# Batch 0 of a block-attention and mixture-of-experts kernel: normalising on GpSimd, an earlier Q load, a later V sum

## The chip, the cores and the metric

One core of one Trainium2 chip. The metric is device time in microseconds of one execution. Engines are named as in the profile: PE (TensorE, its weight loads PEld), DVE (VectorE), ACT (ScalarE), POOL (GpSimd), SP (SyncE, which here only issues DMAs).

## The reference

Three layers, one after another, all in float32:

```python
def attention(q, k, v):                       # (2, 8, 768, 64) each
    k_sum = k.reshape(B, H, 24, 32, D).max(axis=3)      # one summary key per block of 32
    v_sum = v.reshape(B, H, 24, 32, D).mean(axis=3)     # one summary value per block
    scores_l = scale * q @ k.T   where |i - j| < 16, else -1e9
    scores_s = scale * q @ k_sum.T + log(32)
    a = softmax(concat([scores_l, scores_s]))           # exp, divided by (sum + 1e-9)
    return a @ concat([v, v_sum])
x = attention(q, k, v) as (1536, 512)
x = (silu(x @ w_gate) * (x @ w_val)) @ w_out            # d_ff 1536
out = moe2(x)    # 8 experts, top 1, gated: relu(x @ w1[e]) @ w2[e] for each token's expert
```

## The kernel before

Attention runs over sub-blocks s of 64 queries, 12 for each batch. For one sub-block: `att_sm` (line 210) multiplies Q by 96 near keys and 24 summary keys into a PSUM tile S; `att_se` (line 221) runs four pairs of a DVE instruction (mask and row minimum, line 228) and an ACT exponential with its row sum (line 231), giving e; `att_n` (line 235) adds 1e-9 to the sums, takes the reciprocal and multiplies e by it (lines 238 to 240, all on DVE); `att_t` (line 242) transposes e on PE into PT and copies it to pt with ACT; `att_v` (line 252) multiplies by 96 rows of V and 24 rows of V sums that stand under them in the tile vx, and ACT and DVE split the result PV into xh and xl, the transposed input of the dense layer. e has three buffers, so the mask instruction of sub-block s waits for the transposes of s-3.

The order of all this is written out by hand. For batch 0 it is `start` (line 851): loads of six K tiles and three Q tiles; six K stages with filler transposes; three 512 KB loads of V for its block sums (`vs_load`); then the first attention steps, and a loop of 15 turns i in which sub-block i gets its exponentials, i-1 is normalised, i-2 is transposed, i-3 is multiplied by V, and i+2 gets its scores. In the loop also run:

- `q_stage` (line 163): four PE transposes of a loaded Q tile, an ACT copy to qT, and the load of the tile three further on into the buffer that came free. Tile j is transposed in turn 2(j-2), j from 2; it feeds sub-blocks 2j and 2j+1.
- `vs_fold` (line 191): adds V's 16 rows of each half block down to one with four DVE additions of 512, 256, 128 and 64 columns for each of three tiles; `vs_pick` (line 195) adds the halves and places the sums with 20 PE matmuls; `vs_copy` (line 182) brings them into vx with one ACT copy and two GpSimd copies. The first `att_v`, in turn 3, needs them.
- `load_vx` in turns 3 to 11: V rows of sub-block s+3, issued by GpSimd after the product of s has read the buffer.
- `convert` (inside `start`): the weight stream. A unit (256 columns of one weight matrix for all rows) arrives as two 512 KB loads of raw words, is assembled by DVE in three steps (lines 310, 313, 316), written back to DRAM for the second half (line 326), and split by ACT and DVE into whi and wlo (lines 344, 342). `steps` says in which turn each step stands; at the end of a unit's third step the next unit's loads are issued.
- `groups`: from turn 9 PE also runs pieces of the dense layer.

SP issues loads strictly in program order, so a load whose buffer is not yet free holds back those behind it. After `start`, PE runs the dense layer for both halves of the tokens; a step list calls PE work, side work and `pump` (line 348), which assembles and splits one more weight unit when a slot is free. `gate_mm` (line 426) computes one 128x384 tile of gate or value in a PSUM buffer of the pool mm (four buffers; a second pool, at, has four more); `gate_ev` (line 433) reads the pair. `moe1_o` (line 468) accumulates three output tiles O and copies them out with ACT and DVE (line 481, through line 135 and 137).

Of the kernel before, what the change touches and what calls it, by code (L numbers as in the profile page):

```python
# [8 lines left out]
F32 = mybir.dt.float32  # L9
# [4 lines left out]
ALU = mybir.AluOpType  # L14
# [5 lines left out]
class Program:  # L20
# [142 lines left out]
    def q_stage(self, b, i):  # L163
        ps = self.tr_bank(self.qraw.pop((b, i)))
        self.evac(i if self.warm else 1, self.qb(b, i), ps)
        if i < 3:
            self.load_rows("q", b, i + 3)

    def vs_add(self, b, t):
# [65 lines left out]
    def att_n(self, b, s):  # L235
        V = self.nc.vector
        e, st = self.e_t[b, s]
        V.tensor_scalar(out=st[:, 2, :], in0=st[:, 1, :], scalar1=1e-9, scalar2=None, op0=ALU.add)
        V.reciprocal(out=st[:, 2, :], in_=st[:, 2, :])
        V.tensor_tensor(out=e, in0=e, in1=st[:, 2, :].unsqueeze(2).to_broadcast([self.P, 4, 120]), op=ALU.mult)  # L240

    def att_t(self, b, s):
        nc = self.nc
# [157 lines left out]
    def mm3(self, ps, ah, al, bh, bl, start, stop):  # L401
        mm = self.nc.tensor.matmul
        mm(ps, lhsT=ah, rhs=bh, start=start, stop=False)  # L403
        mm(ps, lhsT=ah, rhs=bl, start=False, stop=False)  # L404
        mm(ps, lhsT=al, rhs=bh, start=False, stop=stop)  # L405
# [18 lines left out]
            self.mm3(ps, wh[:, o:o + 128], wl[:, o:o + 128], self.xh[x][:, kc, :n], self.xl[x][:, kc, :n], kc == 0, kc == 3)  # L424

    def gate_mm(self, ids, f, x, nm):
        ps = self.mm_p.tile([self.P, self.TB], F32, tag="mm", name=nm)
        self.project(ps, ids[nm, f // 2], f, x, self.TB)
        if nm == "v" and f % 2 and x == 1:
            self.done(ids["v", f // 2] + 1)  # L430
        return ps
# [419 lines left out]
    def start(self, ids):  # L851

        nc = self.nc
        for i in range(6):
            self.load_rows("k", 0, i)
        for i in range(3):
            self.load_rows("q", 0, i)
        self.fill_t = self.mm_p.tile([self.P, self.P], F32, tag="mm", name="fill")
        self.fill(14)
        for i in range(6):  # L860
            self.k_stage(0, i)
            self.fill(4)
            if i % 2:
                self.vs_load(0, i // 2)
                if i < 5:
                    self.k_edges(i // 2)
        self.load_vx(0, 0)
        self.unit_dma(1)
        self.load_vx(0, 1)
        self.load_vx(0, 2)  # L870
        self.unit_dma(1)
        self.k_sums(0)
        self.q_stage(0, 0)
        self.fill(6)
        self.att_sm(0, 0)
        self.att_sm(0, 1)
        self.q_stage(0, 1)
        self.k_edges(2)
        left, conv, dense, ps = [], [], None, {}

        def convert(first):
            if first:
                conv.append(self.unit_split())
            if next(conv[0], 1):
                conv.pop(0)
                self.unit_dma(1)
        steps = {2: 1, 3: 0, 4: 0, 5: 1, 6: 0, 7: 0, 9: 1, 10: 0, 11: 0}
        groups = {9: 1, 10: 2, 11: 3, 12: 3, 13: 4, 14: 3}
        self.routing_setup()
        for i in range(15):  # L890
            if i < 12:
                self.att_se(0, i)
            if 1 <= i < 13:
                self.att_n(0, i - 1)
            while left:
                left.pop()()
            if i == 14:
                self.gate_ev(ps[0, "g"], ps[0, "v"], 0, 0)
            if i == 1:
                self.k_sums(1)  # L900
            if i == 3:
                self.k_sums(2)
            if i < 2:
                self.vs_fold(((512,), (256, 128, 64))[i])
            if i in steps:
                convert(steps[i])
            if 2 <= i < 14:
                self.att_t(0, i - 2)
            if i >= 3:
                s = i - 3  # L910
                left.append(self.att_v(0, s, self.xh[s // 6], self.xl[s // 6], 64 * (s % 6)))
                if s + 3 < 12:
                    self.load_vx(0, s + 3, nc.gpsimd)
            if i < 10:
                self.att_sm(0, i + 2)
            if i % 2 == 0 and i < 8:
                self.q_stage(0, i // 2 + 2)
            if i == 2:
                self.vs_pick()
            if i >= 3:  # L920
                self.rests()
            if i == 9:
                dense = self.dense_pieces(ids, 0, 0, ps)
            for _ in range(groups.get(i, 0)):
                next(dense)
        left.pop()()
        for _ in dense:
            pass
        self.gate_ev(ps[1, "g"], ps[1, "v"], 1, 0)
        self.unit_dma()  # L930
        self.iota_copies()
# [31 lines left out]
    def main(self):  # L963
        nc = self.nc
        self.setup()
        self.stream_setup()
        self.dense_setup()
        ids = [self.moe1_units(half) for half in range(2)]
        self.attention_setup()
        with self.tc.manual_schedule():  # L970
            self.start(ids[0])
        self.tc.no_sync_barrier()
        self.warm = True
        attB0 = self.att_sides(1, range(6))
        attB1 = self.att_sides(1, range(6, 12))
        prepB = self.prep(1)
        for half in range(2):
            for third in range(3):
                fs = range(4 * third, 4 * third + 4)
                g1 = lambda x, fs=fs: [lambda f=f: self.gate1(ids[half], f, x) for f in fs]  # L980
                g2 = lambda x, f: self.gate2(ids[half], f, x)
                o = lambda x: [lambda f=f: self.moe1_o(ids[half], half, f, x) for f in fs]
                order = [(x, fs[2 * j:2 * j + 2]) for j in range(2) for x in range(2)]
                gs = [st for x, f in order for st in g1(x, f)]
                if (half, third) == (0, 0):
                    self.run(g2(1, 0) + g1(0, fs[2:4]) + g1(1, fs[2:4]) + o(0) + o(1))
                elif (half, third) == (0, 1):
                    self.run(gs + o(0) + o(1), prepB)
                elif (half, third) == (0, 2):
                    self.run(g1(0))  # L990
                    self.run(g2(1, fs[0]) + g2(1, fs[2]), attB0[:4])
                    self.run(o(0) + o(1), attB0[4:], 1)
                elif (half, third) == (1, 0):
                    self.run(g2(0, fs[0]) + g2(0, fs[2]), attB1)
                    self.run(g1(1) + o(0) + o(1), self.lsides(range(6)))
                elif (half, third) == (1, 1):
                    self.run(gs + o(0) + o(1), self.rsides(0))
                    e = self.expert_regs(0)
                    sl = [self.moe2_units(e[0]), self.moe2_units(e[1])]
                    g = self.gathers(0)  # L1000
                else:
                    self.run(gs + o(0))
                    self.run(o(1), self.xsides(g[0:3], 0) + self.lsides(range(6, 9)))
        ls = self.lsides(range(9, 12))
        self.slot(sl[0], 0, self.TS[0][:, 0:3, :], self.xsides(g[3:6], 1) + ls, self.rsides(1)[:5])
        self.run([lambda f=f: self.moe2_f(sl[1], f, 1, self.TB) for f in range(8)], [lambda: self.route_6(1)])
        e = self.expert_regs(1)
        ex = nc.sync.value_load(self.cei[0:1, 0:1], min_val=0, max_val=self.E - 1)
        sl += [self.moe2_units(e[0]), self.moe2_units(e[1]), self.moe2_units(ex)]
        g = self.gathers(1)  # L1010
        self.extra_table(slice(self.NTOK, self.NTOK + 128))
        gx = self.gather(self.idx, self.NTOK, 6)
        y = [lambda f=f: self.moe2_y(sl[1], f, self.TS[0][:, 3:6, :], 3, True) for f in range(8)]
        self.run(y[:3])
        self.run(y[3:], self.xsides(g[0:3], 0), 1)
        self.slot(sl[2], 0, self.TS[1][:, 0:3, :], self.xsides(g[3:6], 1))
        self.slot(sl[3], 1, self.TS[1][:, 3:6, :], [lambda: self.xt_stage(gx, 0, 0)])
        self.more = nc.values_load(self.cei[0:1, self.NCH:self.NCH + 1], min_val=0, max_val=self.NCH)
        self.chunk(sl[4], 0, self.TSx, True)
# [44 lines left out]
```

## Time and profile before

| | us |
|---|---|
| median of 3 runs | 577.37 (574.38 to 577.72) |
| the profiled execution | 574.82, span 573.2 |
| PE busy / DVE / ACT / POOL | 546.8 / 340.7 / 253.6 / 75.2 |
| mean granted TensorE clock | 0.981 of full speed |

The span runs from the first to the last instruction. A matmul's end is modelled, so a busy PE need not be at its peak. Idle time of an engine stands behind its instruction with the engine whose signal ended the wait; a wait for several signals is put down to the one that came last by the profile, which need not be the true one.

### The profile page before, as it was taken

What the parts mean: (1) busy time and instruction counts of PE and PEld (TensorE: products, weight loads), DVE (VectorE), ACT (ScalarE), POOL (GpSimd) and SP (SyncE); (2) the same over time, 40 slices, a digit from 0 to 9 for tenths busy, and PEclk for the clock granted to TensorE, in tenths of its full rate; (3) what the DMA queues carried; (4) which work ended last, traced back from release to release, by engine and by line L of the source; (5) the groups of instructions that cost most, each with busy time, mean ns of one, the idle gap of its engine ahead of it and who ended that gap; (6) DMA issues with size and microseconds to landing.
All of it is one profiled execution on the core that took longest, in us unless ns stands there. A gap on an engine that the chain in (4) does not pass through costs nothing.

```text
span 573.2 us, 9571 instructions
## 1 busy us (share of the span) xinstructions
PE 546.8 (95%) x3566; PEld 498.5 (87%) x3566; DVE 340.7 (59%) x865; ACT 253.6 (44%) x536; POOL 75.2 (13%) x101
## 2 busy tenths in 40 slices
PE   7588999989999999999999999999999999999993
PEld 6466999789989987889989998998998998989892
DVE  5769689989963566663616734334657654625351
ACT  3469634244322785684426331332353444435351
POOL 5022111010000000000000440000000735002020
PEclk9778999999999999999999999999999999999998
DMA  9948699999960254510312233123323387445320
GB/s 191 305 99 245 188 223 301 327 288 313 244 221 0 57 142 117 157 29 13 111 38 73 70 94 133 38 73 129 129 73 111 83 242 254 143 142 168 130 107 4
DMA packets 76769, 83.19 MB, mean 145 GB/s; under 512 B 45023, under 2 KB 55311, under 8 KB 76720
## 3 DMA queue, kind: packets, MB, share of 16 engines
q1 hardware_dynamic: 67936, 72.59, 42.6%
q0 software_dynamic: 8784, 9.96, 7.7%
q8 instruction: 29, 0.48, 0.3%
q14 instruction: 20, 0.16, 0.1%
HBM read 66.76 MB, written 16.03 MB: 144 GB/s over the span
## 4 chain that ended last, share of the span: by engine, by line
PE 80%; DVE 8%; DMA 6%; issue 3%; SPq 1%; ACT 1%; POOL 0%; POOLq 0%; DVEq 0%; ACTq 0%
PE g L403 5%; PE v L403 5%; PE v L404 5%; PE v L405 5%; PE g L405 5%; PE g L404 5%; PE O L403 5%; PE O L405 5%; PE O L404 5%; PE H L403 4%; PE H L405 4%; PE H L404 4%; PE Y L403 4%; PE Y L405 4%; PE Y L404 4%
## 5 line engine op out<-in xcount | busy, mean ns | idle before, releaser
L342 DVE TENSOR_TENSOR wlo<-raw,whi 128x1024 fp32r<-128x1024 f32 x58 | 71.0, 1224 | 77.2 <-ACT whi L344 76.8
L344 ACT CAST whi<-raw 128x1024 fp32r<-128x1024 f32 x58 | 60.9, 1050 | 93.1 <-PE Y L405 30.7
L403 PE MATMUL v<-xh,whi 128*128 128x384 f32 x192 | 65.1, 339 | 2.6 <-ACT part L135 2.6
L403 PE MATMUL g<-xh,whi 128*128 128x384 f32 x192 | 66.3, 345 | 0.0
L405 PE MATMUL g<-xh,wlo 128*128 128x384 f32 x192 | 64.6, 336 | 0.0
L404 PE MATMUL v<-xl,whi 128*128 128x384 f32 x192 | 64.5, 336 | 0.0
L404 PE MATMUL g<-xl,whi 128*128 128x384 f32 x192 | 64.5, 336 | 0.0
L405 PE MATMUL v<-xh,wlo 128*128 128x384 f32 x192 | 64.2, 335 | 0.0
L403 PE MATMUL O<-whi,hh 128*128 128x512 f32 x144 | 58.4, 405 | 0.0
L405 PE MATMUL O<-whi,hl 128*128 128x512 f32 x144 | 56.4, 392 | 0.0
L404 PE MATMUL O<-wlo,hh 128*128 128x512 f32 x144 | 56.3, 391 | 0.0
L437 DVE TENSOR_TENSOR h<-h,v 128x384 f32<-128x384 f32 x48 | 26.5, 552 | 43.9 <-PE v L405 41.3
L336 ACT CAST hh<-h 128x384 fp32r<-128x384 f32 x48 | 24.6, 514 | 60.8 <-DVE h L437 60.6
L657 POOL DMA_INDIRECT tok<-TK,pos x12 | 14.6, 1214 | 256.1 <-DVE big_a L670 152.3
L403 PE MATMUL H<-xh,whi 128*128 128x384 f32 x128 | 43.9, 343 | 0.0
L405 PE MATMUL H<-xh,wlo 128*128 128x384 f32 x128 | 42.9, 335 | 0.0
L404 PE MATMUL H<-xl,whi 128*128 128x384 f32 x128 | 42.8, 335 | 0.0
L231 ACT ACTIVATE e<-e,st 128x120 f32<-128x120 f32 x96 | 36.7, 384 | 10.5 <-DVE st L228 10.4
L403 PE MATMUL Y<-whi,hh 128*128 128x512 f32 x104 | 41.1, 395 | 0.0
L405 PE MATMUL Y<-whi,hl 128*128 128x512 f32 x104 | 40.6, 390 | 0.0
L404 PE MATMUL Y<-wlo,hh 128*128 128x512 f32 x104 | 40.5, 390 | 0.0
L403 PEld LDWEIGHTS v<-xh,whi 128*128 128x128 f32 x192 | 36.0, 188 | 3.4 <-ACT part L135 2.9
(205 smaller groups left out, 1123.4 us busy)
## 6 DMA issues: line engine op xcount, KB each, us to landing
raw<-in_moe_w_dram SPq DMA_DIRECT2D x40, 512.0 KB, 3.6
kept<-w SPq DMA_DIRECT2D x18, 512.0 KB, 4.0
raw<-kept SPq DMA_DIRECT2D x18, 512.0 KB, 3.7
raw<-in_moe_w_gate_dram SPq DMA_DIRECT2D x12, 512.0 KB, 6.0
raw<-in_moe_w_val_dram SPq DMA_DIRECT2D x12, 512.0 KB, 7.2
raw<-in_moe_w_out_dram SPq DMA_DIRECT2D x12, 512.0 KB, 6.4
qkraw<-in_q_dram SPq DMA_DIRECT2D x12, 256.0 KB, 5.6
x2d<-part SPq DMA_DIRECT2D x12, 256.0 KB, 2.3
```

What stands on the lines that cost most here:

```text
L231: nc.scalar.activation(out=e[:, p, :], in_=e[:, p, :], func=AF.Exp, scale=-1.0, bias=st[:, 0, p:p + 1], accum_out=st[:, 1, p:p + 1])
L336: self.nc.scalar.copy(hi, src)
L342: self.nc.vector.tensor_tensor(out=lo, in0=t, in1=hi.bitcast(F32), op=ALU.subtract)
L344: self.nc.scalar.copy(hi, t)
L403: mm(ps, lhsT=ah, rhs=bh, start=start, stop=False)
L404: mm(ps, lhsT=ah, rhs=bl, start=False, stop=False)
L405: mm(ps, lhsT=al, rhs=bh, start=False, stop=stop)
L437: nc.vector.tensor_tensor(out=h, in0=h, in1=V, op=ALU.mult)
L657: ins = nc.gpsimd.indirect_dma_start(out=self.tok[:, :], out_offset=bass.IndirectOffsetOnAxis(ap=self.pos[half][:, i:i + 1], axis=0), in_= ...
```

## The change

Six edits. The multiplication of e by the reciprocal sums goes to GpSimd in batch 0 (`warm` is False only inside `start`). Q tile 3 is loaded right behind the V tiles, ahead of the vx and weight loads; tile 4 ahead of the third vx load and the second weight unit; tile 5 in turn 0, after tile 2 was transposed. `k_sums(0)` and the first `q_stage` are now written ahead of the vx loads, which matters to SP alone. All four folds of V's sums stand in turn 2 and `vs_pick` in turn 3. The conversion steps of the first two weight units stand one turn later. Six gate and value tiles of the dense layer take their PSUM buffer from the pool at.

```diff
--- before.py
+++ after.py
@@ -163,7 +163,7 @@
     def q_stage(self, b, i):
         ps = self.tr_bank(self.qraw.pop((b, i)))
         self.evac(i if self.warm else 1, self.qb(b, i), ps)
-        if i < 3:
+        if i < 3 and self.warm:
             self.load_rows("q", b, i + 3)
 
     def vs_add(self, b, t):
@@ -237,7 +237,8 @@
         e, st = self.e_t[b, s]
         V.tensor_scalar(out=st[:, 2, :], in0=st[:, 1, :], scalar1=1e-9, scalar2=None, op0=ALU.add)
         V.reciprocal(out=st[:, 2, :], in_=st[:, 2, :])
-        V.tensor_tensor(out=e, in0=e, in1=st[:, 2, :].unsqueeze(2).to_broadcast([self.P, 4, 120]), op=ALU.mult)
+        E = V if self.warm else self.nc.gpsimd
+        E.tensor_tensor(out=e, in0=e, in1=st[:, 2, :].unsqueeze(2).to_broadcast([self.P, 4, 120]), op=ALU.mult)
 
     def att_t(self, b, s):
         nc = self.nc
@@ -424,7 +425,8 @@
             self.mm3(ps, wh[:, o:o + 128], wl[:, o:o + 128], self.xh[x][:, kc, :n], self.xl[x][:, kc, :n], kc == 0, kc == 3)
 
     def gate_mm(self, ids, f, x, nm):
-        ps = self.mm_p.tile([self.P, self.TB], F32, tag="mm", name=nm)
+        pool, tag = (self.at_p, "at") if ids is self.ids0 and (x, f) in ((1, 0), (1, 1), (0, 4)) else (self.mm_p, "mm")
+        ps = pool.tile([self.P, self.TB], F32, tag=tag, name=nm)
         self.project(ps, ids[nm, f // 2], f, x, self.TB)
         if nm == "v" and f % 2 and x == 1:
             self.done(ids["v", f // 2] + 1)
@@ -864,17 +866,19 @@
                 self.vs_load(0, i // 2)
                 if i < 5:
                     self.k_edges(i // 2)
+        self.k_sums(0)
+        self.q_stage(0, 0)
+        self.load_rows("q", 0, 3)
         self.load_vx(0, 0)
         self.unit_dma(1)
         self.load_vx(0, 1)
-        self.load_vx(0, 2)
-        self.unit_dma(1)
-        self.k_sums(0)
-        self.q_stage(0, 0)
         self.fill(6)
         self.att_sm(0, 0)
         self.att_sm(0, 1)
         self.q_stage(0, 1)
+        self.load_rows("q", 0, 4)
+        self.load_vx(0, 2)
+        self.unit_dma(1)
         self.k_edges(2)
         left, conv, dense, ps = [], [], None, {}
 
@@ -884,7 +888,7 @@
             if next(conv[0], 1):
                 conv.pop(0)
                 self.unit_dma(1)
-        steps = {2: 1, 3: 0, 4: 0, 5: 1, 6: 0, 7: 0, 9: 1, 10: 0, 11: 0}
+        steps = {3: 1, 4: 0, 5: 0, 6: 1, 7: 0, 8: 0, 9: 1, 10: 0, 11: 0}
         groups = {9: 1, 10: 2, 11: 3, 12: 3, 13: 4, 14: 3}
         self.routing_setup()
         for i in range(15):
@@ -900,12 +904,14 @@
                 self.k_sums(1)
             if i == 3:
                 self.k_sums(2)
-            if i < 2:
-                self.vs_fold(((512,), (256, 128, 64))[i])
+            if i == 2:
+                self.vs_fold((512, 256, 128, 64))
             if i in steps:
                 convert(steps[i])
             if 2 <= i < 14:
                 self.att_t(0, i - 2)
+            if i == 3:
+                self.vs_pick()
             if i >= 3:
                 s = i - 3
                 left.append(self.att_v(0, s, self.xh[s // 6], self.xl[s // 6], 64 * (s % 6)))
@@ -915,8 +921,8 @@
                 self.att_sm(0, i + 2)
             if i % 2 == 0 and i < 8:
                 self.q_stage(0, i // 2 + 2)
-            if i == 2:
-                self.vs_pick()
+                if i == 0:
+                    self.load_rows("q", 0, 5)
             if i >= 3:
                 self.rests()
             if i == 9:
@@ -966,6 +972,7 @@
         self.stream_setup()
         self.dense_setup()
         ids = [self.moe1_units(half) for half in range(2)]
+        self.ids0 = ids[0]
         self.attention_setup()
         with self.tc.manual_schedule():
             self.start(ids[0])
```

## Rows read from the trace of the kernel before

**Rows 1.** The page: engines' busy time (share of span), instructions; TensorE clock in 40 slices.

```profile
PE 546.8 (95%) x3566; PEld 498.5 (87%) x3566; DVE 340.7 (59%) x865; ACT 253.6 (44%) x536; POOL 75.2 (13%) x101
PEclk9778999999999999999999999999999999999998
```

**Rows 2.** Waits of PE from 53 us to the end: total us, times, longest.

```profile
PE v L403 <- ACT part L135: 2.6, 1, 2.6
```

**Rows 3.** Windows: length, busy us of PE, PEld, DVE, ACT, POOL, PEclk, DMA share, GB/s.

```profile
20.00:30.00 10.00, 2.87 (x20) 2.19 (x20) 9.73 (x43) 3.71 (x17) 0.00 (x0) 0.62 1.09 247
30.00:40.00 10.00, 9.48 (x104) 7.92 (x104) 5.09 (x26) 6.12 (x23) 2.77 (x4) 0.70 0.24 60
36.90:55.30 18.40, 15.29 (x227) 12.16 (x225) 18.06 (x74) 16.89 (x65) 4.93 (x7) 0.94 0.78 219
71.00:113.00 42.00, 42.00 (x222) 39.15 (x221) 38.70 (x72) 14.79 (x22) 6.64 (x5) 1.00 1.03 274
```

**Rows 4.** Timeline of PE, 20 to 36 us: start, us, instruction, [idle before <-releaser].

```profile
23.79 1.87 PE L218 MATMUL S<-kx,qT 64*64 64x120 f32 x16
30.52 1.09 PE L130 MATMUL tr<-ident,qkraw 128*128 128x128 f32 x4 [4.87 <-DVE w L313]
31.54 2.33 PE L202 MATMUL vsps<-part,pick 128*24 128x64 f32 x20
34.84 1.12 PE L261 MATMUL PV<-pt,vx 120*64 120x64 f32 x16
```

**Rows 5.** Timeline of SP's DMA issues, 0 to 200 us.

```profile
10.31 2.38 SPq L189 DMA_DIRECT2D part<-in_v_dram  x3
23.00 6.05 SPq L113 DMA_DIRECT2D qkraw<-in_q_dram  x3
```

**Rows 6.** Tile qkraw to 50 us, from issue to landing.

```profile
DMA to landing us min/median/max: 5.5/5.6/5.7
```

**Rows 7.** Groups of DVE by shape, 15 to 55 us: busy, mean ns, idle before.

```profile
L240 DVE TENSOR_TENSOR e<-e,st 128x480 f32<-128x480 f32 x9 | 5.9, 659 | 0.3
```

**Rows 8.** Timeline, all engines, 12 to 37 us.

```profile
12.57 0.66 PE L130 MATMUL tr<-ident,qkraw 128*128 128x128 f32 x4 [0.64 <-DMA qkraw<-in_q_dram]
18.68 0.58 ACT L135 COPY qT<-tr 128x512 f32<-128x512 f32 x1 [0.20 <-PE tr L130]
19.07 1.76 DVE L193 TENSOR_TENSOR part<-part 128x1536 f32<-128x1536 f32 x1 [3.07 <-DMA vx<-in_v_dram]
22.82 1.94 DVE L193 TENSOR_TENSOR part<-part 128x768 f32<-128x768 f32 x3
34.95 0.28 DVE L228 CUSTOM_DVE_ANT_0 e<-S,mask 128x120 f32<-128x120 f32 x1 [4.45 <-PE PT L247]
36.90 0.41 ACT L231 ACTIVATE e<-e,st 128x120 f32<-128x120 f32 x1
```

**Rows 9.** Groups of POOL by shape, 0 to 70 us.

```profile
L121 POOL DMA_DIRECT2D vx<-in_v_dram x9 | 7.1, 784 | 18.2 <-PE PV L261 16.7 <-DMA vx<-in_v_dram 1.5
L185 POOL COPY vx<-vx 24x512 f32<-24x512 f32 x2 | 1.2, 608 | 24.6 <-ACT vx L183 24.6
L507 POOL TENSOR_SCALAR_AFFINE_SELECT tri<-tri 128x128 f32<-128x128 f32 x1 | 0.3, 287 | 0.1
```

**Rows 10.** Timelines of PE, ACT and DVE, 104 to 127 us.

```profile
114.84 1.04 ACT L344 CAST whi<-w 128x1024 fp32r<-128x1024 f32 x1 [5.47 <-DVE r_pre L603]
115.79 1.07 ACT L135 COPY part<-O 128x512 f32<-128x512 f32 x2
116.42 0.44 PE L403 MATMUL v<-xh,whi 128*128 128x384 f32 x1 [2.61 <-ACT part L135]
126.58 0.55 DVE L437 TENSOR_TENSOR h<-h,v 128x384 f32<-128x384 f32 x1
```

**Rows 11.** Timeline of DVE, 66 to 120 us.

```profile
70.49 0.56 DVE L437 TENSOR_TENSOR h<-h,v 128x384 f32<-128x384 f32 x1 [0.99 <-PE v L405]
71.65 0.76 DVE L310 TENSOR_SCALAR w<-raw 128x512 uint32<-128x512 uint32 x2
```

## The prediction

> **What bounds the kernel now.** I read the page first, then the waits of PE, then windows by stage, then the timelines of the stage that the change touches. The page shows PE busy for 95% of the span, with its long spell of a low clock near the start [rows 1]. From 53 us to the end PE waits once for long, 2.6 us [rows 2]. So this kernel is a start of 55 us in which PE has too little to do, then about 520 us in which PE sets the pace. What shortens the start, or takes away that wait, shortens the whole, provided that nothing else PE needs (the weight stream above all) stays where it was.
>
> In the start the window from 20 to 30 us is DVE's (9.73 of 10), the one from 30 to 40 is nobody's (DVE 5.09, ACT 6.12, DMA share 0.24) [rows 3]. PE's timeline shows why: the scores end at 25.66 and the next transposes begin only at 30.52, after 4.87 us of idle; `vs_pick` follows at 31.54 and the first product with V at 34.84 [rows 4]. Those transposes read Q tile 3. The releaser named is a weight conversion on DVE with which they share no data, so I look for a DMA: SP issued this tile's load no earlier than 23.00, behind vx and four weight loads [rows 5]; a Q load takes 5.6 us from issue to landing [rows 6], which gives at least 28.6, with the DMA engines full (share 1.09) [rows 3]. I take this load for the releaser. Behind it DVE stands idle 4.45 us, because its mask instruction at 34.95 needs an e buffer whose transposes are queued behind Q's, and ACT reaches the exponentials of turn 4 only at 36.90 [rows 8]. From there to 55.30, where the dense layer starts, DVE is busy 18.06 of 18.40 us and ACT 16.89 [rows 3].
>
> **The change part by part.**
>
> *Q tile 3 behind V.* Its buffer is free when tile 0 has been transposed, at 13.23 [rows 8]; SP is through with issuing V's loads at 12.69 [rows 5], so SP waits half a microsecond while its transfers still run. V's loads end DVE's wait at 19.07 [rows 8]; 256 KB more at 247 GB/s [rows 3] take 1.06 us, so tile 3 is there at about 20 instead of after 28.6. What it and tile 4 are moved past comes later by one such transfer (vx 0 and 1, unit 0: 1.1) or two (vx 2, unit 1: 2.1). Unit 0 is first read in turn 3, unit 1 in turn 6, both a turn later in count than before; I cost this at nothing, covered by the later steps. If that cover is gone, DVE waits up to 2.1.
>
> *Folds in turn 2.* DVE no longer waits 3.1 us for V, but this doesn't turn into time: turn 2's normalising needs the exponentials of turn 1 on ACT, which follow the qT copy that ends at 19.26 and take 1.5 us, to 20.8. Adding and reciprocal end at 21.2, and then all folds, 1.76 and 1.94 us, at 24.9; now they end at 24.76 [rows 8]. A loss of 0.1. Turn 3's mask instruction stands behind them, as turn 2's did.
>
> *What the two give together.* `vs_pick` can start at 24.95 instead of 31.54; its 2.33 us, 0.6 of ACT's copy and two signals put the first product with V at 27.9 instead of 34.84, 6.9 earlier [rows 4]. ACT's copy of that product and then turn 4's exponentials come at 29.5 instead of 36.90, 7.4 earlier [rows 8]: there too the product went just ahead of them. [...] So 6.9.
>
> *The multiplication on GpSimd.* It takes 0.66 us off DVE in every turn [rows 7]. Some 5.5 turns of 3.3 us lie between 36.90 and 55.30, so DVE would fall from 18.06 to 14.4 there. ACT, whose 16.89 us stay, is then the next bound [rows 3]: at most 1.5 us more. The price on GpSimd is in no row. Below: its copy of 512 columns took 608 ns, which for 480 columns is 0.57. Above: an affine select of 128 columns took 287 ns, in proportion 1.08 for 480 [rows 9]. I take 1.08, since this instruction has two inputs. With a DMA issue of 0.78 [rows 9] that is 1.9 us of a turn, and PE wants e only a turn later: it is hidden. Queued behind it on GpSimd is a vx load three turns ahead of its use. If the cover is gone, PE's transposes wait, and through the three buffers of e DVE does. I take 0 for this edit, between 1.5 gained and 3.4 lost (the first rival). [...]
>
> *PSUM buffers from the pool at.* The 2.6 us stall of PE is a value tile that waits for an O tile to be copied out; ACT does that at 115.79 only, because ahead of it stands the split of a weight unit for which it had waited 5.47 us [rows 10]. With both tiles of that pair in the other pool, the next claim on an O buffer comes two tiles of 2.1 us later than 113.8, at 118, when ACT's copies are over. So 2.6 is removed. What is late next: DVE's multiplication at 126.58 [rows 10], which frees the buffer of a value tile that PE would want again at about 127 in the new order (six tiles and a transposition after 113.8). That is thin; I charge 0.3 and take 2.3 (bounds 0 and 2.6). The other four tiles cost nothing: PE doesn't wait there now [rows 2].
>
> *Conversion a turn later.* The first two units end in turns 5 and 8; unit 2 keeps turns 9 to 11, and its raw words are asked for at the end of turn 5. Nothing, with four turns between.
>
> **Sum.** 6.9 + 2.3 = 9.2 us off 574.82 is 565.6. That execution was 2.55 below the median of 577.37, near the fastest of the three runs. I put the median of the changed kernel between the two readings, at 566.5.
>
> **Rivals.**
>
> *The gain in the start is shrunk by DVE and GpSimd getting in each other's way.* No GpSimd computation here runs beside a DVE instruction with two SBUF inputs, so the rows don't say. As a mechanism: each multiplication (1.08) holds back DVE's folds or weight assembly for its length, and takes 0.66 off. In 5.5 turns that is 2.3 us more on DVE, with 1.1 more in the folds: 3.4 of the 6.9 are gone, 569.0 on the profiled execution, up to 571.6 for a median. For it: the multiplication starts just as DVE goes on to those instructions. Against it: DVE gets slack to ACT. [...]
>
> *The weight stream gives it back.* From 71 to 113 us the DMA share is 1.03 and DVE is busy 38.7 of 42 [rows 3]. If the stream stayed where it is, ACT would still be held to 114.84 [rows 10] and PE, come earlier, would wait there: 573 to 577, no change. Against it: the assembly at 71.65 follows directly on an instruction that had waited for PE [rows 11], so the stream's clock is PE's, and it moves along.
>
> *Slower: GpSimd becomes the bound of the loop.* Place: its in-order queue in turns 3 to 11, with multiplication, vx issue and the wait for PE's product. It decides from a GpSimd turn longer than the 3.3 us of now. To be 1% slower the nine turns must give back 9.2 and 5.8 more, 1.7 each, a turn of 5.0: a multiplication of over 4 us, 583 us. That is four times the upper bound, and GpSimd waited 16.7 us for PE in that stretch [rows 9].
>
> **Chances.** 1% (5.8 us) is about what a measurement tells from no change. Forecast 0.62, own range 562 to 569; first rival 0.20, mostly still 1% faster; weight stream 0.11; slower 0.07. Faster 0.78, same 0.15, slower 0.07. The range is 562 to 572: at the lower end 1.5 more from the loop and a fast set of runs; at the upper the first rival.
>
> **What would show it.** Right: Q's transposes in turn 2 without a wait; `vs_pick` at about 25 us; the first dense product near 48; no wait of PE for ACT's copy of O; GpSimd's multiplications near 1.1 us. Wrong: PE waiting for GpSimd before PT, DVE's folds or conversions much longer than now, or the stall at 113 back in another place.

## The result and the profile after

The changed kernel takes 568.81 us (median of 4 runs, 568.48 to 569.39) where the kernel before takes 575.88 in the same comparison: a ratio of 0.9882 (95% interval 0.9834 to 0.9930), 7.07 us or 1.2% faster. The profiled execution takes 568.94 us with a span of 567.3, 5.88 less than the one before. Forecast were 566.5 (562 to 572) and, on the profiled execution, a gain of 9.2.

The page of the changed kernel, the lines that answer to [rows 1]:

```profile
PE 544.8 (96%) x3566; PEld 495.5 (87%) x3566; DVE 341.5 (60%) x853; ACT 252.7 (45%) x536; POOL 87.8 (15%) x113
PEclk9998999999999999999999999999999999999998
```

In this execution the low clock of the first slices is nearly gone; the second profiled execution of the same kernel has it again (0.51 of full speed from 24 to 34 us, below), so the change alone doesn't remove it. The timeline of PE, where [rows 4] had a wait of 4.87 us before Q tile 3, and the start of the dense layer:

```profile
21.51 0.63 PE L130 MATMUL tr<-ident,qkraw 128*128 128x128 f32 x4 [0.34 <-DMA qkraw<-in_q_dram]
25.21 1.30 PE L202 MATMUL vsps<-part,pick 128*24 128x64 f32 x20 [1.15 <-DVE part L193]
28.13 0.69 PE L262 MATMUL PV<-pt,vx 120*64 120x64 f32 x16 [1.63 <-ACT vx L183]
...
48.11 0.69 PE L404 MATMUL g<-xh,whi 128*128 128x384 f32 x1
```

Q tile 3 now makes PE wait 0.34 us, the sums are picked at 25.21 (forecast 24.95), the first product with V comes at 28.13 (27.9), the dense layer at 48.11 instead of 55.30. So far, and in this execution, the forecast holds to 0.3 us. The waits of PE from 45 us to the end (total us, times, longest), where [rows 2] had the one of 2.6:

```profile
PE PT L248 <- POOL e L241: 1.2, 1, 1.2
PE v L404 <- DVE h L439: 1.0, 1, 1.0
PE PV L262 <- DVE st L228: 0.8, 1, 0.8
PE S L218 <- DVE st L228: 0.7, 1, 0.7
PE O L404 <- DVE part L485: 0.5, 1, 0.5
```

The wait for ACT's copy of O is gone. Five smaller ones stand there, all behind DVE or GpSimd; the first, third and fourth lie in the loop, the other two, 1.0 and 0.5 us, are new in the dense layer. The timeline of POOL and, below it, of DVE in turns 1 to 5 shows where both lose time:

```profile
18.50 0.99 POOL L241 TENSOR_TENSOR e<-e,st 128x480 f32<-128x480 f32 x1 [8.47 <-DVE st L239]
20.80 2.56 POOL L241 TENSOR_TENSOR e<-e,st 128x480 f32<-128x480 f32 x1 [1.31 <-DVE st L239]
```

```profile
20.75 4.40 DVE L193 TENSOR_TENSOR part<-part 128x1536 f32<-128x1536 f32 x4
...
26.42 1.54 DVE L311 TENSOR_SCALAR w<-raw 128x512 uint32<-128x512 uint32 x2
```

The first multiplication on GpSimd takes 0.99 us. The second one starts 0.05 us after DVE's first fold, of 1.76, and takes 2.56, and the next fold takes 1.62 where it takes 0.96 without work on GpSimd (e1). I read that as one waiting for the other; the four folds take 4.40 us instead of 3.70 [rows 8]. The groups of DVE by shape, 15 to 50 us (busy, mean ns, idle before), say the same of the weight conversion:

```profile
L311 DVE TENSOR_SCALAR w<-raw 128x512 uint32<-128x512 uint32 x6 | 5.3, 926 | 0.0
L317 DVE SCALAR_TENSOR_TENSOR w<-raw,w 128x512 uint32<-128x512 uint32 x4 | 4.5, 1170 | 0.0
L314 DVE SCALAR_TENSOR_TENSOR w<-raw,w 128x512 uint32<-128x512 uint32 x4 | 3.4, 880 | 0.0
L193 DVE TENSOR_TENSOR part<-part 128x768 f32<-128x768 f32 x1 | 1.6, 1624 | 0.0
```

**PE's lead.** To see where time goes I count PE's matmuls, the same 3566 in the same order in both kernels: the lead at the nth is how much earlier it starts than in the kernel before, each counted from its first matmul. The columns are the 181st, 461st, 801st, 821st, 901st, 1101st and 3001st, by the time of the kernel before: pick, loop's end, before and after the 2.6 us wait, then three places in the dense layer and behind it. The column on the right is the granted TensorE clock of that execution from 24 to 34 us, as a share of full speed.

```
us in the kernel before     33    57   110   116   130   168   458   clock
kernel before              0.0   0.0   0.0   0.0   0.0   0.0   0.0    0.50
changed kernel             7.1   6.0   5.7   8.5   7.2   5.9   5.8    1.00
changed kernel, again      6.7   4.1   3.8   6.6   6.7   5.9   5.9    0.51
e1  multiply on DVE        7.2   5.3   5.4   8.1   8.2   6.4   6.4    0.51
e2  only Q loads           3.4   2.4   2.4   3.3   3.2   3.2   3.2    0.69
e3  only GpSimd           -0.2  -2.0  -2.0  -0.2  -0.2  -0.2  -0.2    0.50
e4  only PSUM pool         0.3   0.7   0.7   3.5   3.6   3.1   3.1    0.50
e5  without pool           7.0   4.8   3.5   4.5   4.5   4.5   4.5    0.66
e6  conversion first       7.1   8.7   5.3   8.1   5.5   3.8   3.8    1.00
e7  less DMA               7.1   6.0   5.7   8.5   8.6   8.6   8.6    1.00
e8  less DVE               7.0   5.8   5.6   8.3   7.8   7.8   7.8    1.00
e9  folds back             3.0   0.8  -0.7   2.1   2.1   0.8   0.7    0.75
e10 DVE, one fold first    6.8   5.1   5.1   7.9   7.7   6.3   6.3    0.51
e12 stream early           7.5   5.8   3.0   5.8   5.4   5.3   5.3    0.66
```

The changed kernel wins 7.1 us at the pick, loses 1.4 to the loop's end and just behind, wins 2.8 at 113 us, and loses 2.6 of it again between 117 and 165 us. From there on nothing changes. 0.4 to 0.9 us of each lead was there at the 131st matmul, ahead of what the edits touch: K and the first Q tile arrived earlier in these executions.

The executions also differ in the clock, and that bears on what their leads say of the loop. The windows of the changed kernel, first and second execution (columns as in [rows 3]):

```profile
24.00:34.00 10.00, 7.22 (x123) 6.13 (x124) 9.64 (x42) 6.72 (x27) 6.59 (x8) 1.00 0.86 212
24.00:34.00 10.00, 8.19 (x82) 6.93 (x82) 8.93 (x40) 5.51 (x21) 4.81 (x6) 0.51 0.78 194
```

One kernel was granted 1.00 of full speed there in one execution and 0.51 in the other, though from 20 to 24 us PE had been busy 2.38 and 2.35 us; why is not shown. At the pick the two leads still differ by 0.4 us only; the dense layer starts at 48.11 and, in the second execution, 49.55:

```profile
49.55 0.44 PE L404 MATMUL g<-xh,whi 128*128 128x384 f32 x1
```

So up to 57 us e6, e7 and e8 compare with the first execution, e1 and e10 with the second.

### The profile page after: what moved, and what is told of

Read it like the earlier page. It is cut to its first block, busy times and chain, and to the rows that moved or that the text cites. A ratio compares the mean times of both kernels' runs of the same rounds, so it can differ in the third digit from the quotient of the medians.

```text
span 567.3 us, 9590 instructions
## 1 busy us (share of the span) xinstructions
PE 544.8 (96%) x3566; PEld 495.5 (87%) x3566; DVE 341.5 (60%) x853; ACT 252.7 (45%) x536; POOL 87.8 (15%) x113
## 4 chain that ended last, share of the span: by engine, by line
PE 74%; DVE 10%; DMA 7%; issue 4%; ACT 1%; SPq 1%; POOL 1%; POOLq 0%; DVEq 0%
PE v L404 5%; PE O L404 5%; PE v L405 5%; PE g L404 4%; PE v L406 4%; PE O L406 4%; PE O L405 4%; PE g L406 4%; PE g L405 4%; PE H L404 4%; PE H L406 4%; PE H L405 4%; PE Y L404 4%; PE Y L406 4%; PE Y L405 4%
## 5 line engine op out<-in xcount | busy, mean ns | idle before, releaser
L659 POOL DMA_INDIRECT tok<-TK,pos x12 | 13.4, 1113 | 256.1 <-DVE big_a L672 152.2
```

The lines of the kernel that those rows point to most:

```text
L659: ins = nc.gpsimd.indirect_dma_start(out=self.tok[:, :], out_offset=bass.IndirectOffsetOnAxis(ap=self.pos[half][:, i:i + 1], axis=0), in_= ...
```

## The experiments

Each row of the table above is the profiled execution of one kernel; ratios are those of the runs to the kernel before.

**e1: the multiplication back on DVE.**

```diff
-        E = V if self.warm else self.nc.gpsimd
-        E.tensor_tensor(out=e, ...
+        V.tensor_tensor(out=e, ...
```

> The changed kernel with the multiplication of e back on DVE, all else kept. Theory A (DVE and GpSimd shut each other out): the conversion steps of 128x512 words go back from 0.93 to 1.17 us each to 0.42 to 0.68, the folds from 4.40 to 3.70 us, and DVE pays 0.6 us a turn for the multiplication; in sum the dense layer starts 0 to 1.5 us earlier than with the change, and the 1.2 us lost between its start and the end of the loop come back: 566 to 568 against 568.9. Theory B (GpSimd relieves DVE as intended): six turns lose 0.6 us each, so 3 to 4 us slower, 572.

567.40 us, ratio 0.9874 (0.9847 to 0.9901). DVE's groups, 15 to 55 us:

```profile
L313 DVE SCALAR_TENSOR_TENSOR w<-raw,w 128x512 uint32<-128x512 uint32 x6 | 3.8, 682 | 0.0
L316 DVE SCALAR_TENSOR_TENSOR w<-raw,w 128x512 uint32<-128x512 uint32 x4 | 2.6, 682 | 0.0
L310 DVE TENSOR_SCALAR w<-raw 128x512 uint32<-128x512 uint32 x6 | 2.3, 420 | 0.0
L193 DVE TENSOR_TENSOR part<-part 128x768 f32<-128x768 f32 x1 | 1.0, 957 | 0.0
```

The conversions are back at 0.42 and 0.68, the fold at 0.96. Theory B fails: the multiplication on GpSimd relieves nothing. The ratio is 0.0008 below that of the change and 0.0033 below that of its repetition (e11), which is 0.5 and 1.9 us; the intervals overlap (0.9834 to 0.9930 and 0.9880 to 0.9935), so the sign is likely, the size open. The dense layer starts at 48.70: 0.85 us earlier than in the second execution of the changed kernel, which had the same low clock, 0.4 of it K's arrival, and 0.6 later than in the first, which had the full clock. Theory A's earlier start is there in part.

**e2: the new order of Q loads alone**, put into the kernel before; folds, multiplication, conversions and pools as they were.

```diff
+        self.k_sums(0); self.q_stage(0, 0); self.load_rows("q", 0, 3)   # ahead of load_vx(0, 0)
...
+        self.load_rows("q", 0, 4)           # ahead of load_vx(0, 2)
...
+                if i == 0: self.load_rows("q", 0, 5)
```

> The kernel before with the new order of loads alone (Q tiles 3, 4, 5 early). Theory A (the whole gain is Q tile 3's wait): the product with V that needs the sums starts near 28 us instead of 34.84, the dense layer near 48, PE stays 7 us ahead to the end: 568 where the kernel before takes 575, a ratio of 0.988. Rival: without the later folds DVE's wait for V takes the place of the wait removed, and less than 4 us remain, a ratio over 0.993.

570.85 us, ratio 0.9933 (0.9906 to 0.9959): the rival. DVE's timeline and PE's waits from 70 us:

```profile
20.53 1.76 DVE L193 TENSOR_TENSOR part<-part 128x1536 f32<-128x1536 f32 x1 [5.44 <-DMA vx<-in_v_dram]
```

```profile
PE v L403 <- ACT part L135: 1.7, 1, 1.7
```

With Q's wait removed, DVE's wait for V in turn 0, 5.44 us in front of everything that DVE does next, is what ends last: the lead at the pick is 3.4 instead of 7.1.

**e3: the multiplication on GpSimd alone**, in the kernel before (the edit of e1 the other way round).

> The kernel before with the multiplication on GpSimd alone. Theory A (mutual exclusion): Q's wait at 25 to 30 us is untouched, and the turns after it get 0.3 to 0.6 us longer on DVE through conversions of 0.9 to 1.2 us: 1 to 3 us slower. Theory B: DVE relieved, 1 to 2 us faster, up to ACT's bound.

574.85 us, ratio 1.0012 (0.9988 to 1.0036). PE's timeline:

```profile
24.78 1.11 PE L248 MATMUL PT<-ident,e 128*120 128x128 f32 x4 [5.96 <-POOL e L241]
25.82 1.87 PE L218 MATMUL S<-kx,qT 64*64 64x120 f32 x16
30.73 1.09 PE L130 MATMUL tr<-ident,qkraw 128*128 128x128 f32 x4 [3.04 <-DVE w L314]
```

The loop ends 2.0 us later at the same granted clock as before (0.50 from 24 to 34 us), as theory A has it. But the end is the same, for PE then waits 0.8 us instead of 2.6 at 113: being late costs nothing there, since ACT's copy stands at 115.98 (115.79 before [rows 10]).

**e4: the other PSUM pool alone**, in the kernel before.

```diff
-        ps = self.mm_p.tile([self.P, self.TB], F32, tag="mm", name=nm)
+        pool, tag = (self.at_p, "at") if ids is self.ids0 and (x, f) in ((1, 0), (1, 1), (0, 4)) else (self.mm_p, "mm")
+        ps = pool.tile([self.P, self.TB], F32, tag=tag, name=nm)
```

> The kernel before with the six PSUM tiles in the other pool alone. Theory C (DVE and ACT behind the weight stream hold PE in this stage, the buffer only said where): the 2.61 us wait at 113 us goes, and waits for DVE's product h and others between 117 and 165 us give at least 2 of it back: 0 to 0.6 us faster. Rival (the buffer was the cause): PE keeps 2 us or more, 572.5 to 573 on a run of 574.8.

572.77 us, ratio 0.998 (0.9958 to 1.0002), and in the profile PE keeps 2.4 of the 2.8 us that it gains at 113. Theory C as I put it fails here: alone, the buffer was the cause. (The interval of the ratio just reaches no change, so this rests on the profile.) This profile also names the releaser that I had inferred for [rows 4]:

```profile
30.19 1.09 PE L130 MATMUL tr<-ident,qkraw 128*128 128x128 f32 x4 [3.90 <-DMA qkraw<-in_q_dram]
```

**e5: the change without the pool.** The diff of e4 the other way round, in the changed kernel.

> The changed kernel with the six gate and value tiles back in the pool mm. Theory C (PE can't get further ahead of the weight stream than some 3 us, whichever buffer is in the way): a wait of about 2 us for ACT's copy of O comes back near 108 us, the waits for DVE after it go away, and the time is that of the changed kernel within 0.5 us, 568.5 to 569.5. Rival (the pool's 2.6 us are a gain of their own, as I forecast): 2 us or more slower, 571.

570.84 us, ratio 0.9929 (0.9903 to 0.9955), against 0.9882 and, run again in e11, 0.9907 with the pool. PE's timeline:

```profile
111.91 0.45 PE L404 MATMUL v<-xh,whi 128*128 128x384 f32 x1 [1.57 <-ACT part L135]
```

The wait is back and the later ones are gone, as theory C says; the ratios are 1.3 to 2.7 us apart, as the rival says, though the lead of this execution was 2.2 us shorter at 110 us already, with a granted clock of 0.66 from 24 to 34 us and of 0.57 from 52 to 56. The intervals overlap: the pool's worth inside the change lies between 0 and 2.7 us, and the runs don't fix it better.

**e6: conversion ahead of normalising in each turn**, in the changed kernel.

```diff
-            if 1 <= i < 13:
-                self.att_n(0, i - 1)
...
             if i in steps:
                 convert(steps[i])
+            if 1 <= i < 13:
+                self.att_n(0, i - 1)
```

> The changed kernel with the conversion step of a turn written ahead of the normalising, so that GpSimd's multiplication runs beside instructions that read PSUM. Theory A (two SBUF inputs, or a packed form, of DVE and GpSimd's reading shut each other out): steps of 0.42 and 0.68 us again where they are 0.93 to 1.17 now, GpSimd at 0.99 each, turns 0.5 us shorter from turn 4 on, the dense layer starting 1 to 2 us earlier: 566.5 to 568. Rival (the conversions are slow because their raw words are still landing, or for another reason): the steps stay slow and the time stays at 568.9. The folds of turn 2 keep their place and their 4.4 us in both.

568.99 us, ratio 0.9897 (0.9870 to 0.9924). DVE's groups, 15 to 55 us, and PE's waits from 70 us:

```profile
L317 DVE SCALAR_TENSOR_TENSOR w<-raw,w 128x512 uint32<-128x512 uint32 x6 | 3.9, 684 | 0.0
L314 DVE SCALAR_TENSOR_TENSOR w<-raw,w 128x512 uint32<-128x512 uint32 x6 | 3.9, 683 | 0.0
L311 DVE TENSOR_SCALAR w<-raw 128x512 uint32<-128x512 uint32 x6 | 2.6, 468 | 0.0
```

```profile
PE v L404 <- DVE h L439: 1.8, 1, 1.8
PE v L404 <- ACT part L135: 0.5, 1, 0.5
```

Same instructions, same GpSimd work, another neighbour: the steps are fast again, 0.68 and 0.47 us instead of 0.88 to 1.17. That settles the cause of the slow conversions: the work on GpSimd beside them. Which property of a step counts is not shown; the steps of two inputs and the shift of one (line 311) were slow alike. GpSimd's multiplications did not all come to the expected 0.99 (1.34 on average): four of twelve took 1.78 to 2.55 us, one beside a fold and three beside DVE's split of a weight unit (line 343). The loop gains 2.7 us of lead on the changed kernel (8.7 at its last turns) at the same full clock and loses 3.4 just behind, where PE waits 1.5 us for vx loads and the clock was 0.70 from 52 to 56 us. Of the 4.3 us lost behind 116 us, 2.3 are the two waits shown; 1.7 went while the granted clock was 0.50 from 125.28 to 128.69 us, right behind the wait of 1.8. This execution, 570.98, is the slowest of its six, so its end says little; the median has no gain either.

**e7 and e8: the weight stream made lighter**, in the changed kernel.

```diff
# e7, in vs_add
+        if 0 < t < 7:
+            return
# e8, in convert, ahead of the third step
+        if self.warm:
+            return
```

> The changed kernel without six of the eight loads by GpSimd that add up V's rows for batch 1's block sums (those sums are left incomplete), 1.2 MB of DMA less between 60 and 165 us. Theory C1 (DMA sets the pace of the weight stream there): the stream's write-backs come 1.5 to 3 us earlier at 150 us, PE waits no more after 113, and PE stays 1.5 us or more further ahead at 165: 566.5 to 567.5. Theory C2 (DVE sets it): PE's lead at 165 us stays within 0.5 us of the changed kernel's, 568.5.

> The changed kernel without the third conversion step from the fourth weight unit on (the lowest three bits of those weights are left out), 1.2 us of DVE less for each of 15 units. Theory C2 (DVE sets the pace from 71 to 165 us, busy 92%): PE's waits for DVE near 118 and 157 us go, and PE stays 1.5 us or more further ahead: 566 to 567.5. Theory C1 (DMA): the stream's write-backs come at the same times and PE keeps at most 0.5 us more.

With less DMA PE keeps all of its lead: 8.5 at 116 us, 8.6 at 168, not one wait from 70 us on. (With the sums of batch 1 incomplete the result is another one, and PE runs 3986 matmuls instead of 3566 in 727.92 us, so e7 is read up to 458 us only, where the order is the same.) With less DVE work it keeps 7.8, and what it loses is a wait of 0.5 us for a K tile's load, not for DVE; the median, 567.92 with a ratio of 0.9883 (0.9851 to 0.9915), does not resolve that from the change. Each theory expected the other's run to show nothing, and both runs moved: the write-back at 152.18 us in the changed kernel comes at 148.72 in e7 and 148.58 in e8, and DVE's waits for DMA from 70 to 170 us fall from 5.6 us in all to 1.7 in e7. DVE's conversions wait for raw words, and the products that PE needs wait behind the conversions, as two lines of DVE in the changed kernel show, between which it never stands idle:

```profile
116.77 0.43 DVE L311 TENSOR_SCALAR w<-raw 128x512 uint32<-128x512 uint32 x1 [0.91 <-DMA raw<-in_moe_w_gate_dram]
...
122.13 0.56 DVE L439 TENSOR_TENSOR h<-h,v 128x384 f32<-128x384 f32 x1
```

PE's wait for that product ends at 122.74. What holds PE there is this one queue, fed by DMA.

**e9: the folds back in turns 0 and 1**, the pick in turn 2, in the changed kernel.

```diff
-            if i == 2:
-                self.vs_fold((512, 256, 128, 64))
+            if i < 2:
+                self.vs_fold(((512,), (256, 128, 64))[i])
```

> The changed kernel with V's folds back in turns 0 and 1 and the pick in turn 2. Theory A (V's loads now land 1.5 us later because Q tile 3 shares the engines, and folds in an early turn put that wait in front of everything DVE does): DVE idle near 5 us before the first fold, the first product with V near 31 us instead of 28.1, the dense layer 2 to 3.5 us later than with the change; 0.5 to 3 us slower in the end, since the weight stream hides a part. My forecast (the move of the folds is worth nothing): the same within 0.5 us at the first product.

574.10 us, ratio 0.9989 (0.9970 to 1.0008): the whole gain is gone, more than I expected. DVE's and PE's timelines:

```profile
20.49 1.76 DVE L193 TENSOR_TENSOR part<-part 128x1536 f32<-128x1536 f32 x1 [5.03 <-DMA vx<-in_v_dram]
```

```profile
25.36 1.11 PE L248 MATMUL PT<-ident,e 128*120 128x128 f32 x4 [6.30 <-POOL e L241]
...
31.10 0.69 PE L262 MATMUL PV<-pt,vx 120*64 120x64 f32 x16
```

The reason that I gave, Q's load sharing the engines with V's, is at most 0.8 us of it: with the old order of loads the first fold began at 19.91 (e3) and 19.71 (e4), and 19.07 in [rows 8] was an early one.

**e10: multiplication on DVE as in e1, and the 512-column fold ahead of turn 2's normalising** (the other three stay behind it).

```diff
+            if i == 2:
+                self.vs_fold((512,))
             if 1 <= i < 13:
                 self.att_n(0, i - 1)
```

> The multiplication back on DVE, and the first of the four folds ahead of turn 2's normalising, where DVE waits for ACT: folds of 3.7 us that end about 24 us, the first product with V near 27 instead of 27.8 in the kernel with the multiplication on DVE alone. Theory A with C1: dense layer up to 1 us earlier, the end 0 to 1 us earlier, 566 to 567.5, a ratio near 0.986. Rival (the weight stream takes all of it): the same as with the multiplication on DVE, 567.4.

568.17 us, ratio 0.9886 (0.9857 to 0.9916): the rival, no gain over e1. The pick starts at 25.24, 0.4 later than in e1 (24.80) at the same granted clock of 0.51: ahead of it in PE's queue stand turn 2's transposes, which start at 23.43 after 1.26 us of waiting for DVE's normalising, and the fold is now ahead of that normalising.

**e11: the changed kernel again.**

> The changed kernel, unaltered, on the chip of the two others, to compare with: 568 to 569.5, a ratio of 0.987 to 0.99; the profile shows how far two executions of one kernel differ at the dense layer's start and at 165 us (1 us, from the arrival of K and of the weights).

569.39 us, ratio 0.9907 (0.9880 to 0.9935). Two profiled executions of one kernel have leads of 6.0 and 4.1 at the loop's end, and 5.9 both at 168 us: a difference of 1.9 us in the start, which goes with the clock of 1.00 and 0.51 there, is lost in the dense layer.

**e12: e1 with the fourth weight unit converted in turns 12 to 14.**

```diff
-        steps = {..., 9: 1, 10: 0, 11: 0}
+        steps = {..., 9: 1, 10: 0, 11: 0, 12: 1, 13: 0, 14: 0}
```

> The multiplication back on DVE, as in e1, and the fourth weight unit converted in turns 12 to 14 of the loop instead of after it, so that its raw buffers come free 3 to 5 us earlier and the loads behind it fill a stretch in which the DMA share was 0.14 to 0.3. Theory C1 (the weight stream sets PE's place at 165 us): the stream's write-backs from the fourth on come 2 to 4 us earlier, PE loses nothing after 113 and ends 1 to 2 us ahead of e1: 565 to 566.5, a ratio of 0.984. Rival (the stream is not the limit, DVE in the loop is): DVE's extra 3.2 us in turns 12 to 14 hold PE in the loop, the same 567.4 or slower.

569.27 us, ratio 0.9910 (0.9888 to 0.9933): no gain over e1 and likely slower, a miss. The window from 71 to 113 us (columns as in [rows 3]) and PE's waits from 70 us:

```profile
71.00:113.00 42.00, 39.74 (x206) 36.26 (x205) 36.71 (x64) 14.69 (x23) 6.59 (x5) 1.00 1.11 306
```

```profile
PE v L403 <- DVE h L438: 2.3, 2, 1.6
```

The unit's write-back came 5.5 us earlier than in e1 (63.95 against 69.48), the last one 0.4 later (156.93 against 156.50). The DMA share of the window, 1.11, is that of e1 (1.10), so the stream as a whole is no faster. The product that ends PE's wait of 1.6 us started on DVE at 84.27, directly behind four conversion steps from 81.86 on.

## Why the prediction was right, and where it was not

*Q tile 3.* Right: at 30.5 PE had waited for that load, and now it doesn't. Alone the edit is worth about half of what I gave the pair (e2: 3.2 us of lead at the end).

*Folds in turn 2, a loss of 0.1.* Wrong as the price of the edit. I compared the end of the folds before and after (24.76, forecast 24.9, measured 25.15), which is right, but not with the kernel that has the other edits and not this one. There, V's wait is what ends last; the move is worth 4.7 us in the medians (e9 against e11). The two edits only pay together.

*The two together, 6.9.* Right in this execution: 7.19 at the dense layer's start (55.30 to 48.11), 0.5 of it K's earlier arrival. Part of that is luck: I had counted with the low clock of the kernel before (`vs_pick` 2.33 us, here 1.30, in the second execution 2.33), and the execution with such a clock starts the dense layer at 49.55, 5.75 earlier than before. No run shows by itself the 0.5 that lies between the 7.4 of turn 4's exponentials and the 6.9; those exponentials came at 29.13 instead of 36.90 here, 7.8 earlier. Behind the start 1.5 us were lost by 72 us, which I had not charged; 0.8 of it is PE's wait for DVE's mask instruction. The wait of 1.2 us for GpSimd's e came ahead of the start, at 44.73.

*The multiplication, 0.* Its own length was right (0.99 undisturbed, taken as 1.08), and so was the first rival's mechanism (folds of 4.40 us in all instead of 3.70, two-input steps of 0.88 and 1.17 instead of 0.68), to which I gave 0.20. The window that answers to the third of [rows 3] has DVE still full, so ACT never became the bound:

```profile
28.90:49.30 20.40, 16.87 (x244) 13.49 (x243) 20.03 (x71) 17.13 (x65) 12.25 (x14) 0.95 0.70 207
```

By the ratios of e1 its price is 0.5 to 1.9 us, not the rival's 3.4. Alone, in the kernel before, it made the loop 2.0 us longer and the whole no slower (e3): the dense layer behind takes up much of what the loop gains or loses.

*The pool, 2.3.* The step that failed: "What is late next: DVE's multiplication ... I charge 0.3", and with it "the stream's clock is PE's, and it moves along", which I had read off one instruction at 71.65. The place was right:

```profile
122.74 0.45 PE L404 MATMUL v<-xh,whi 128*128 128x384 f32 x1 [0.98 <-DVE h L439]
```

The size was not: of 2.8 us gained, 2.6 were lost by 168 us. This is the second rival in part, to which I gave 0.11: the stream moved along, but its write-backs were 4.4 to 5.7 us earlier between 69 and 128 us while PE was up to 8.5. Taking load off the stream gives the rest back (e7, e8).

The traces give the limit too. The kernel before had 2.8 us in hand there: the product at 126.58 [rows 10] ends at 127.13, and PE's tile starts at 129.94. At an O tile of the dense layer it had 1.2: DVE is done with the buffer at 158.27, and the tile starts at 159.42. The table takes PE's lead and subtracts how much earlier the stream's nearest write-back came (127.76 and 157.34 in the kernel before), in front of each tile and behind it:

```
                        at 130 us        at 159 us
                       front behind     front behind
changed kernel         4.1   2.8       2.3   1.2
changed kernel, again  2.2   2.2       2.0   1.2
e1  multiply on DVE    2.5   2.5       2.3   1.2
e4  only PSUM pool     1.9   1.9       1.7   1.2
e6  conversion first   4.7   2.8       0.9   0.9
e9  folds back         2.9   2.8       2.2   1.2
e10 DVE, one fold      3.1   2.8       2.3   1.2
```

Whatever PE is further ahead of the stream than 2.8 and then 1.2 us is lost there; e2, e3 and e5 stay below 0.7 and lose nothing. That is why the pool alone keeps most of its gain (e4), and why both executions of the changed kernel end at 5.9: their streams are 4.7 us earlier at the second place.

So of 9.2 us forecast 5.9 came: 0.3 more in the start, 2.1 missing in the pool's term, and the loss of 1.5 between the dense layer's start and 72 us not seen. The median 568.81 lies inside the range because that reached for the first rival, whose mechanism came true while most of the loss came from the stream. The signs that I had named for being wrong (PE waiting for GpSimd, longer folds and conversions, the stall back in another place) all showed, though the time stayed in the range.

## What to carry to other kernels

Price an edit against the kernel that has all the others and lacks it, not against the kernel before: a wait that two edits share goes only with both. Here a stall was removed ahead of a queue that is nearly always busy (DVE, 37.22 of 42 us from 71 to 113), and the gain stayed only as far as that queue moved along. Look in the trace at how long each result of the queue lies ready before it is used: here 2.8 and 1.2 us, and no more could be kept. Before work goes to GpSimd, look at which instructions of DVE will stand beside it: here steps of 0.68 us became 0.88 and 1.17 on average. And compare the granted clock of two executions before their difference is put down to an edit.

## What the runs showed of the hardware

DVE and GpSimd held each other up. Beside a GpSimd multiplication of two SBUF inputs, DVE's two-input steps took 0.88 and 1.17 us on average instead of 0.68 (e1), its one-input shift 0.93 instead of 0.42, a fold 1.62 instead of 0.96; the multiplication itself 0.99 to 2.56. The one of 2.56 started 0.05 us behind a fold of 1.76. In another order (e6) DVE's steps have 0.68 and 0.47.

The granted clock of TensorE did not repeat: two executions of one kernel, with PE busy 2.38 and 2.35 us of the 4 before, had 1.00 and 0.51 of full speed from 24 to 34 us.
